# Backward loads in pieces of up to 512 KB instead of 256 KB, and a padded weight loaded from a copy

## The chip, the cores and the metric

The kernel runs on one core of one Trainium2 chip. The metric is the device time of one execution in microseconds (us). A profile is one execution taken by the hardware profiler; its span can differ by some us from the timed runs of the same kernel. Kernels sent together ran on one chip and share its runs of the kernel before; across those chips the median of the kernel before was 1447.5, 1449.6, 1453.8 and 1451.4 us, so kernels of different groups are compared by their ratios. A ratio is the mean time of one kernel's fast runs over that of the kernel before in the same rounds, so it is not quite the ratio of the medians quoted beside it.

Engines: PE multiplies matrices (PEld is its weight load), DVE, ACT and POOL work element by element, SP issues most DMAs. The 16 DMA engines move the data.

## The reference, cut to what matters

A block with attention and a gated feed-forward network side by side, in bf16, and all its gradients: S = 2048 tokens, D = 448, 16 heads of 28, F = 1792.

```python
xn = layernorm(x)
out = x + mha(xn, wqkv, wo) + (silu(xn @ w_gate) * (xn @ w_up)) @ w_down
# returned: out and, for a given grad_out, the gradients of
# x, wqkv, wo, w_gate, w_up, w_down
```

## The kernel before: the parts that the change and the argument touch

The forward (to about 610 us) computes attention and the feed-forward net and stores what the backward will need in DRAM: q, k and the like (QD_d, KD_d), feed-forward tiles (F_d), attention output (OT_d), transposed weights (wT_d). The backward then runs 512 attention steps. Each needs PE (two score and two gradient matmuls, four accumulating ones), ACT (two exponentials) and DVE (two products, the ds tile). Between the steps PE is filled with other units: y (the output of the block), dx (gradient through the feed-forward net), dc (through the projections).

All loads of the backward are issued by one queue, SP, between the DMA transposes of ds:

```python
RATE = 100 << 10                        # bytes a step

def drip(key, pieces, due):             # put pieces on the waiting list
    slow.extend((due, key, o, i) for o, i in pieces)
    slow.sort(key=lambda x: x[0])

def drop():                             # once a step
    # ... rate = RATE, or more where a piece is due soon
    credit += rate
    while slow and credit > 0:
        _, _, o, i = slow.pop(0)
        SP.dma_start(out=o, in_=i)
        credit -= size(o)

def load_q(g, qc):
    t = new_q(g, qc)                    # [P, 4, 512] bf16, 512 KB
    drip(("q", g, qc), [(t[:, i:i + 2], QD_d[g, qc, :, i:i + 2]) for i in (0, 2)], 128 * g + 4 * qc - 4)

def dst_dma(b, ds, qi):                 # three of four steps: transpose by DMA
    if qi == 0:
        dsT[b] = bk.tile([P, 4, 2, 4, P], BF16, name="dsT", bufs=3)
    SP.dma_start_transpose(out=dsT[b][:, qi].rearrange("p j kt s -> p (j kt) s"),
                           in_=ds[:].rearrange("p j k -> p (j k)"))
# ... the ds of the fourth step is transposed by PE and copied by ACT
# ds_sb has 10 buffers; y has 2
```

The weight wo is needed with each head of 28 rows padded to 32. The kernel before loads it in the backward in four DMAs of 28 partitions, into a tile that POOL clears first. The forward had built the same padded layout in SBUF once already (wo_pad).

The softmax here doesn't subtract the row's maximum and nothing guards it: scores larger than these inputs give would overflow.

## Time and profile before

| | kernel before |
|---|---|
| time | 1447.26 us (1446.37 to 1447.65, 3 runs) |
| profiled span | 1448.2 us |
| PE, ACT, DVE busy | 92%, 87%, 80% |
| DMA packets, bytes | 701763, 271.18 MB |
| plain DMAs and transposes on SP | 558 and 505 (compiled order) |

The busy row of an engine says how long it ran instructions, the waits say what ended its idle time. The DMA row is the mean share of time in which each of the 16 engines had a packet under way; packets overlap, so it can pass 1. The lines themselves are shown in the prediction.

### The profile page before, as it was taken

The page shows a single profiled execution, that of the slowest core. Times are in us where ns is not written, and L with a number is a line of the kernel's source. Part 1 is how long each engine was busy: PE and PEld are TensorE (multiplying, and loading weights), DVE is VectorE, ACT ScalarE, POOL GpSimd, SP SyncE. Part 2 cuts the span into 40 slices and gives each one's busy share as a digit, 9 for nine tenths or more (in the row PEclk, how much of TensorE's full clock was granted, in tenths as well). Part 3 has the DMA queues.
Part 4 walks back from the last instruction along what each step waited for, and adds up shares of the span by engine and source line. Part 5 has one row for each costly group of instructions (what it writes and reads, how often), then busy time and mean ns, then how long its engine had stood idle before and what let it go on. Part 6 is the DMA issues. An engine that isn't in the chain of part 4 may idle for free. (4 is left out here: it accounts for less than half of the span.)

```text
span 1448.2 us, 34787 instructions
## 1 busy us (share of the span) xinstructions
PE 1335.4 (92%) x12708; PEld 539.9 (37%) x12708; DVE 1151.7 (80%) x1997; ACT 1261.2 (87%) x2193; POOL 363.1 (25%) x486
## 2 busy tenths in 40 slices
PE   5899999999999999889899989999999999999996
PEld 2333333333333333333333433433343344443343
DVE  6677756666667666488898988888889999989988
ACT  5788988988999999778898988899989999989974
POOL 6475514453344453110101101101001011010005
PEclk9999999999999999989999999999999999999998
DMA  6797947796778676799999999999999999999971
GB/s 153 161 211 184 220 112 166 177 203 154 157 170 184 143 175 145 193 211 204 217 218 211 208 225 181 211 211 212 232 193 192 208 215 230 199 197 201 204 145 60
DMA packets 701763, 271.18 MB, mean 187 GB/s; under 512 B 620224, under 2 KB 676248, under 8 KB 701592
## 3 DMA queue, kind: packets, MB, share of 16 engines
q1 hardware_dynamic: 696616, 262.83, 88.5%
q0 software_dynamic: 3568, 5.83, 1.8%
q8 instruction: 100, 1.64, 0.5%
q14 instruction: 71, 0.58, 0.1%
q10 hardware_dynamic: 1408, 0.30, 0.1%
HBM read 65.04 MB, written 59.90 MB: 86 GB/s over the span
## 5 line engine op out<-in xcount | busy, mean ns | idle before, releaser
L840 DVE TENSOR_TENSOR ds_sb<-db,e_sb 128x512 bf16<-128x512 f32 x1024 | 646.8, 684 | 54.7 <-issue 25.5
L834 ACT ACTIVATE e_sb<-sb 128x512 bf16<-128x512 f32 x1024 | 555.0, 612 | 66.1 <-PE db L818 49.8
L611 ACT ACTIVATE eT<-s_w 128x1024 bf16<-128x1024 f32 x256 | 263.5, 1029 | 47.0 <-PE s_ps L608 44.0
L613 ACT ACTIVATE eT<-s_ps 128x512 bf16<-128x512 f32 x512 | 280.5, 613 | 0.0
L818 PE MATMUL db<-kd,qd 32*128 32x512 bf16 x1024 | 236.1, 385 | 7.2 <-DVE ds_sb L840 6.4
L810 PE MATMUL sb<-kd,qd 32*128 32x512 bf16 x1024 | 210.7, 388 | 7.4 <-DMA qd<-QD_d 3.5
L959 POOL TENSOR_TENSOR dq_acc<-dq_acc,dq_st 128x256 f32<-128x256 f32 x64 | 46.4, 726 | 571.6 <-ACT dq_st L957 571.6
L917 PE MATMUL acc<-ds_sb,qd 128*32 128x512 bf16 x1024 | 161.1, 391 | 0.0
L913 PE MATMUL acc<-e_sb,qd 128*32 128x512 bf16 x1024 | 159.0, 391 | 1.3 <-DVE dw_o L527 1.3
L900 ACT COPY dsT<-db 128x1024 bf16<-128x1024 bf16 x128 | 130.2, 1017 | 14.1 <-PE db L895 13.5
L379 POOL TENSOR_TENSOR nn<-nn,ag 128x512 f32<-128x512 f32 x56 | 71.2, 1271 | 249.6 <-DVE ag L377 240.9
L608 PE MATMUL s_ps<-QQ,KK 32*128 32x512 bf16 x512 | 125.3, 385 | 3.9
L1127 PE MATMUL genb<-wguT,dau_c 128*128 128x448 bf16 x448 | 117.5, 355 | 6.3 <-ACT dq_st L957 3.9
L608 PE MATMUL s_w<-QQ,KK 32*128 32x512 bf16 x512 | 100.3, 387 | 11.8 <-ACT eT L611 10.2
L810 PEld LDWEIGHTS <-qd 32*128 32x128 bf16 x1024 | 48.2, 91 | 152.4 <-issue 140.6
L420 PE MATMUL gen<-xn_t,f_sp 128*128 128x448 bf16 x416 | 91.8, 354 | 2.6 <-DVE nn L394 1.7
L944 PE MATMUL genb<-dsT,kd 128*32 128x256 bf16 x2048 | 79.1, 274 | 6.0 <-DVE y L1079 4.2
L420 PEld LDWEIGHTS <-f_sp 128*128 128x128 bf16 x640 | 55.7, 98 | 75.9 <-issue 32.0
L895 PE MATMUL db<-ident_bf,ds_sb 128*128 128x128 bf16 x1032 | 79.0, 220 | 1.1 <-DVE ds_sb L840 1.1
L895 PEld LDWEIGHTS <-ds_sb 128*128 128x128 bf16 x1032 | 67.9, 98 | 24.6 <-issue 6.0
L380 POOL TENSOR_TENSOR nn<-nn,tt 128x512 f32<-128x512 f32 x56 | 72.0, 1286 | 4.4
L450 PE MATMUL gen<-eT,VS 128*32 128x512 bf16 x1024 | 68.4, 384 | 4.3 <-DVE nn L394 2.2
(163 smaller groups left out, 1879.5 us busy)
## 6 DMA issues: line engine op xcount, KB each, us to landing
F_d<-hda SPq DMA_DIRECT2D x56, 384.0 KB
dau_c<-F_d SPq DMA_DIRECT2D x56, 256.0 KB
h_c<-F_d SPq DMA_DIRECT2D x24, 256.0 KB
qd<-QD_d SPq DMA_DIRECT2D x24, 256.0 KB
dsT<-ds_sb SPq DMA_TRANSPOSE x383
dc<-dqkvT_d SPq DMA_DIRECT2D x12, 384.0 KB
wT_d<-wT_f SPq DMA_DIRECT2D x14, 256.0 KB
KD_d<-qk_sp SPq DMA_DIRECT2D x7, 512.0 KB
```

The costliest lines, as they stand in the source:

```text
L420: PE.matmul(ps[:, :D], lhsT=fsp[fc][:, t // 4, w, t % 4, :], rhs=rhs[:, t, :], start=(t == 0), stop=(t == NT - 1))
L608: PE.matmul(sp4[hh], lhsT=KK[g][r:r + HP, kt * P:(kt + 1) * P], rhs=QQ[g][r:r + HP, qsl], start=True, stop=True, tile_position=(r, 0))
L611: ACTE.activation(out=e2[0][:], in_=wide[:], func=ACT.Exp, scale=SCALE)
L613: ACTE.activation(out=e2[1][:, j], in_=sp4[2 + j], func=ACT.Exp, scale=SCALE)
L810: PE.matmul(s_ps[:], lhsT=qside[g, qc][r:r + HP, 0, qi * P:(qi + 1) * P], rhs=kside[g, kc][r:r + HP, 0, :], start=True, stop=True, tile_po ...
L818: PE.matmul(d_ps[:], lhsT=qside[g, qc][r:r + HP, 1, qi * P:(qi + 1) * P], rhs=kside[g, kc][r:r + HP, 1, :], start=True, stop=True, tile_po ...
L834: ACTE.activation(out=est[k][:, j], in_=sps.pop((k, j))[:], func=ACT.Exp, scale=SCALE)
L840: DVE.tensor_tensor(out=ds[:, j], in0=dps.pop((k - 1, j))[:], in1=est[k - 1][:, j], op=ALU.mult)
L895: PE.transpose(ps[:, c, :], ds[:, c // 4, (c % 4) * P:(c % 4 + 1) * P], ident_bf[:])
L900: ACTE.copy(out=o, in_=ps[:])
L913: PE.matmul(a[r:r + HP, :], lhsT=sp4[:, 1, r:r + HP], rhs=e[:, j, :], start=first, stop=last, tile_position=(0, r), skip_group_check=True)
L917: PE.matmul(a[r:r + HP, :], lhsT=sp4[:, 0, r:r + HP], rhs=ds[:, j, :], start=first, stop=last, tile_position=(0, r), skip_group_check=True)
```

## The change

Its intent: fewer and larger transfers, as the DMA row is full in the backward, with no change to the order of any compute engine. Pieces of 256 KB become pieces of up to 512 KB; wo is stored once, padded, in the forward, and comes back in one DMA. Cut to its core:

```diff
+    wo_d = dram.tile([P, G, D], BF16)
 ...
         if k == 13:
             woT_load(3)
+            SP.dma_start(out=wo_d[:], in_=wo_pad[:, :, :D])
 ...
-        drip(("q", g, qc), [(t[:, i:i + 2], QD_d[g, qc, :, i:i + 2]) for i in (0, 2)], 128 * g + 4 * qc - 4)
+        drip(("q", g, qc), [(t[:], QD_d[g, qc])], 128 * g + 4 * qc - 4)
 ...  (k, fT, x_c, o_c, wd and wguT alike)
-                               for a, b in ((0, 2), (2, 4), (4, 6), (6, 7))], due)      # h_c
+                               for a, b in ((0, 4), (4, 7))], due)
-    POOL.memset(wo_sb[:], 0.0)
-    drip(("y", 0, 1), [(wo_sb[HP * pv(hh):HP * pv(hh) + DH, :, :], wo_v[hh]) for hh in range(4)], 50)
+    drip(("y", 0, 1), [(wo_sb[:], wo_d[:])], 50)
-        drip(("dx", ch, fq), [(d[:, i - f0], F_d[ch, :, i, 1:3, :]) for i in range(f0, f1)], now + 16)
+        drip(("dx", ch, fq), [(d[:, i - f0:min(i + 2, f1) - f0], F_d[ch, :, i:min(i + 2, f1), 1:3, :]) for i in range(f0, f1, 2)], now + 16)
```

More of the change, by code (lines that the diff above doesn't have):

```diff
@@ L776, in load_q @@
         t = new_q(g, qc)
-        drip(("q", g, qc), [(t[:, i:i + 2], QD_d[g, qc, :, i:i + 2]) for i in (0, 2)], 128 * g + 4 * qc - 4)
+        drip(("q", g, qc), [(t[:], QD_d[g, qc])], 128 * g + 4 * qc - 4)
     def load_k(g, kc):
         t = new_k(g, kc)
-        drip(("k", g, kc), [(t[:, 0:2], KD_d[g, kc, :, 0:2]), (t[:, 2], KD_d[g, kc, :, 2])], 128 * g + 16 * kc - 4)
+        drip(("k", g, kc), [(t[:], KD_d[g, kc])], 128 * g + 16 * kc - 4)
     steps = [(g, hp, kc, qc, qi) for g in range(G) for hp in range(2) for kc in range(4)
@@ L871 @@
     w2 = bk.tile([P, 4, 2, P], BF16, name="dqT", bufs=1)
-    drip(("f",), [(fT[:, sc], fT_d[:, sc]) for sc in range(4)], 10)
+    drip(("f",), [(fT[:, a:a + 2], fT_d[:, a:a + 2]) for a in (0, 2)], 10)
     def late_dw(c):
@@ L1038, in load_y @@
             x_c = yp.tile([P, 4, D], BF16, name="x_c")
-            drip(("y", ch, half), [(x_c[:, a:a + 2], x_d[:, 4 * ch + a:4 * ch + a + 2, :]) for a in (0, 2)], due)
+            drip(("y", ch, half), [(x_c[:], x_d[:, 4 * ch:4 * ch + 4, :])], due)
             ych[ch, 2] = x_c
@@ L1042, in load_y @@
             o_c = yp.tile([P, G, 512], BF16, name="o_c")
-            drip(("y", ch, half), [(o_c[:, a:a + 2], OT_d[ch, :, a:a + 2]) for a in (0, 2)], due)
+            drip(("y", ch, half), [(o_c[:], OT_d[ch])], due)
             ych[ch, 3] = o_c
@@ L1047 @@
     wo_sb = yp.tile([P, G, D], BF16, name="wo_sb", bufs=1)
-    POOL.memset(wo_sb[:], 0.0)
     wd_v = B_w_down.rearrange("(fc p) d -> p fc d", p=P)
-    drip(("y", 0, 0), [(wd_sb[:, a:a + 2, :], wd_v[:, a:a + 2, :]) for a in (0, 2, 4, 6)], 35)
+    drip(("y", 0, 0), [(wd_sb[:, a:a + 4, :], wd_v[:, a:a + 4, :]) for a in (0, 4)], 35)
     load_y(0, 0)
     load_k(0, 2)
-    drip(("y", 0, 1), [(wd_sb[:, a:a + 2, :], wd_v[:, a:a + 2, :]) for a in (8, 10, 12)], 50)
-    drip(("y", 0, 1), [(wo_sb[HP * pv(hh):HP * pv(hh) + DH, :, :], wo_v[hh]) for hh in range(4)], 50)
+    drip(("y", 0, 1), [(wd_sb[:, a:a + 3, :], wd_v[:, a:a + 3, :]) for a in (8, 11)], 50)
+    drip(("y", 0, 1), [(wo_sb[:], wo_d[:])], 50)
     load_y(0, 1)
@@ L1104, in load_w @@
         w = dxs["w", fq] = dxs["pool"].tile([P, 5, 2, D], BF16, name="wguT")
-        drip(("dx", 0, fq), [(w[:, i - f0], wT_d[:, i, :, :D]) for i in range(f0, f1)], due)
+        drip(("dx", 0, fq), [(w[:, i - f0:min(i + 2, f1) - f0], wT_d[:, i:min(i + 2, f1), :, :D]) for i in range(f0, f1, 2)], due)
     def load_dx(ch, fq):
```

## The prediction

> **What bounds the kernel now.** I read the busy times and the 40 slices first, then the busy time by stretch, then who waits for a DMA, then the DMA queue's own rows. The chain that ended last is no help: it covers the final 1.5 us only.
>
> ```profile
> PE 1335.4 (92%) x12708; PEld 539.9 (37%) x12708; DVE 1151.7 (80%) x1997; ACT 1261.2 (87%) x2193; POOL 363.1 (25%) x486
> PE   5899999999999999889899989999999999999996
> DMA  6797947796778676799999999999999999999971
> ```
>
> The reader sees two rows at 9: PE from start to end, and the mean of the 16 DMA engines from slice 18 on, where the backward begins. That second row is what the change aims at, so I took the backward apart (columns: stretch, length, busy us of PE, PEld, DVE, ACT, POOL, granted clock, DMA share, GB/s):
>
> ```profile
> 650.00:700.00 50.00, 45.92 (x495) 17.53 (x492) 42.09 (x69) 43.74 (x83) 4.35 (x6) 0.93 1.06 205
> 950.00:1000.00 50.00, 47.60 (x536) 19.44 (x534) 40.76 (x66) 47.39 (x93) 4.36 (x6) 1.00 1.15 220
> 600.00:1400.00 800.00, 751.86 (x8492) 313.24 (x8492) 711.10 (x1192) 714.99 (x1329) 67.83 (x94) 0.99 1.07 206
> ```
>
> From 600 to 1400 us PE is busy 752 of 800 us (94%), with ACT and DVE at 89%. The DMA share is 1.07: packets overlap in time, so a share over 1 says that the engines always have work queued, not that anyone waits. Who waits is in the wait view (us in total, times, longest), from which these are all the waits of compute engines for DMAs in the backward:
>
> ```profile
> DVE y L1079 <- DMA out_dram<-y: 5.7, 3, 2.3
> DVE ds_sb L840 <- DMA dsT<-ds_sb: 5.0, 6, 1.7
> PEld L810 <- DMA qd<-QD_d: 3.6, 1, 3.6
> PE sb L810 <- DMA qd<-QD_d: 3.5, 1, 3.5
> PEld L810 <- DMA kd<-KD_d: 2.5, 1, 2.5
> PE sb L810 <- DMA kd<-KD_d: 2.0, 1, 2.0
> PEld L1071 <- DMA o_c<-OT_d: 1.3, 1, 1.3
> PEld L944 <- DMA dsT<-ds_sb: 1.2, 2, 0.9
> PE genb L1071 <- DMA o_c<-OT_d: 0.8, 1, 0.8
> PEld L1071 <- DMA dsT<-ds_sb: 0.4, 1, 0.4
> PEld L810 <- DMA dsT<-ds_sb: 0.4, 1, 0.4
> ```
>
> PE lost 3.5 + 2.0 + 0.8 = 6.3 us to DMAs, the 3.5 of it at the very turn (before 625 us) on a load that the change leaves as it is. DVE lost 10.7 us, all between 640 and 900 us; from 900 us on only 0.4 us of a weight load's wait is left. So although the DMA row is full, **PE with ACT and DVE close behind** bounds the backward, and DMA is a full but tolerated second.
>
> Last the queue that issues: is SP late?
>
> ```profile
> SPq L827 <- DVE ds_sb L840: 270.8, 244, 2.5
> SPq L827 <- PE db L818: 97.9, 86, 2.9
> L827 SPq DMA_TRANSPOSE dsT<-ds_sb x383: 1231/1267/3143, 624.3 to 1400.5; - x192
> L767 SPq DMA_DIRECT2D dau_c<-F_d x56: 421/572/1197, 913.6 to 1243.1; - x56
> ```
>
> The rows give min/median/max ns of one issue. A transpose holds the queue 1.27 us, a load 0.57 us. But the two waits ahead say that the queue stood 369 us waiting for the ds tile that the next transpose reads: it keeps pace with the compute and has room.
>
> **What the Trainium skill says.** "Perfetto Trace Analysis", section "DMA Optimizations", says that larger DMAs use memory bandwidth better and that DMAs under 2 KB have large overhead, but also that splitting lets some start sooner. The first is the change's intent; the second is what it gives up. "DMA: Bandwidth & Descriptors", section "Why small descriptors are slow (HBM only)", gives about 3 cycles a packet beside one per 32 bytes: estimated from that page, 67 cycles against 64 at 2 KB and 131 against 128 at 4 KB, so 2 KB to 4 KB saves some 2%. No row of the trace before shows it. "Issuing engines are not separate DMA queues" on the same page has all DMAs interleave on the same 16 engines: a transpose shares them with a load, whatever its size. The trace agrees that transposes get late when loads are heavy (DVE waits 5.0 us for ds_sb to be read, only during 640 to 900 us).
>
> **The change part by part.** I compared the compiled instruction order of both kernels. PE (25288 rows), DVE (1032) and ACT (1152) are the same row for row; POOL loses one row; SP goes from 1065 to 978 DMAs. So nothing moves on the bounding engines, only the times at which data is there.
>
> 1. *Fewer issues.* Loads: dau_c 56 to 32, h_c 32 to 16, kd 28 to 14, qd 24 to 12, wguT 14 to 8, o_c 8 to 4, x_c 8 to 4, wd 7 to 4, fT 4 to 2, wo 4 to 1; and one store more. That is 88 less and 1 more: 87 x 0.57 us = 50 us of the SP queue. All of it lies beside other work: SP waits 369 us for producers, and will wait some 50 us more. On the path: 0.
>
> 2. *The same bytes.* Only qd, kd, o_c and fT get longer contiguous runs per partition (2 KB to 4 KB; kd 2 + 1 to 3). They are 24 x 256 KB + 14 x 384 KB + 8 x 256 KB + 4 x 256 KB = 14.2 MB, a twentieth of the 271 MB moved; h_c keeps runs of 1 KB, dau_c of 2 KB, wd and x_c of 0.9 KB. At 2% that is 14.2 MB / 206 GB/s x 0.02 = 1.4 us of DMA time over the whole backward. On the path: under 1.
>
> 3. *When a load is complete.* The drip sends a piece as soon as its credit is above zero and then goes into debt, so a whole tile goes out where its first half went before. Counting dsT transposes ahead of each load, most tiles are complete 1 to 3 transposes earlier (a transpose each 2 us: 776 us / 383). The kd load that PE waits 2.0 us for (at 843.5 us; its second piece issued only at 841.1) had 101 and 102 transposes ahead, and now has 100; the o_c load of the 0.8 us wait is likewise complete some two transposes earlier. Both waits should go: 2.0 + 0.8 = 2.8 us at most, on PE.
>
> 4. *What stands behind a larger piece.* At 206 GB/s 256 KB take 1.27 us and 512 KB 2.54 us, so a transpose, a store of y or a small load queued behind one can land 1.3 us later, half as often. The dsT tile is read at least 9 steps after its transposes are issued, (1400 - 615) / 512 = 1.53 us each, or 14 us: hidden. The tight places are the 6 ds_sb and 3 y waits on DVE, 10.7 us. They could grow by 1.3 us each, 9 x 1.3 = 12 us on DVE, or shrink, as the mean traffic is equal. DVE has 11% of slack, so I take +1 us on the end.
>
> 5. *wo.* The four loads of 28 partitions (98 KB each, 0.9 KB runs) become one of 448 KB over 128 partitions with 3.5 KB runs: four issues of 0.39 us to one, no wait on either. The POOL memset of 1.61 us at 626 us goes; POOL is idle there and nobody waited for it. The new store of 448 KB is issued at about 65 us, next to the last woT transpose; there the DMA share is 1.02 at 214 GB/s, so it takes 459 KB / 214 GB/s = 2.1 us and can hold up the weight transpose behind it. PE is busy 16.75 of 20 us there. I take +0.3 us.
>
> Sum: 0 - 0.5 - 2.8 + 1 + 0.3 = -2.0 us: 1447.26 - 2.0 = **1445 us**.
>
> **The rivals.** (a) *The DMA engines are the real bound*: share 1.07 to 1.15, and if large pieces were much cheaper the backward would shorten as a whole. Against it: the waits above, and that PE is at 95% precisely where the share is 1.15. If all the 6.3 + 10.7 us went, and PE got all of it, 1430 us. (b) *Bursts delay transposes*: 512 KB at once ahead of tight waits; for it, those waits exist already. All 12 us of step 4 on the path would give 1458; more only if PE starts to wait for dsT, which the 14 us of lead speak against. (c) *All hidden*: every wait moves to another place and the end stays at 1447. That is close to my own answer.
>
> **Range and chances.** I choose 1445, with 1438 (DVE's waits shrink too) to 1453 (half of rival b). A change of 2% needs 29 us. That is more than all DMA waits taken together, so faster gets 0.02; slower needs a new steady wait for transposes, 0.02; within 2%, 0.96.
>
> **What would show it.** Right: SP with 87 fewer DMAs and longer waits for ds_sb; PE's kd and o_c waits gone; PE's busy time between 600 and 1400 us unchanged, about 752; DMA share still over 1. Step 4 shows in DVE's waits on dsT and y, between 5 and 20 us. Wrong: PE waiting for dsT for tens of us, or the DMA share clearly lower with the span shorter by as much, would say that the transfers bounded it after all; a later start of the backward (first row of L810 now at 614.6 us) by over 2 us would say that step 5 was mis-sized.

## The result, and the profile after

The changed kernel took 1447.89 us (1447.69 to 1448.04, 4 runs) beside 1447.45 us for the kernel before on the same chip (1446.37 to 1451.47, 4 runs): ratio 0.9998, 95% interval 0.9979 to 1.0017. It is the same time. The profiled span was 1445.9 us.

The busy rows in 40 slices, and the busy time by stretch, of the changed kernel:

```profile
PE   5899999989999999889898999999999999999996
DMA  5897857696778676799999999999999999999971
```

```profile
650.00:700.00 50.00, 46.17 (x493) 18.07 (x492) 42.53 (x70) 44.39 (x84) 4.78 (x7) 0.90 1.13 213
950.00:1000.00 50.00, 47.62 (x552) 19.80 (x555) 41.32 (x66) 47.73 (x93) 4.36 (x6) 1.00 1.14 210
600.00:1400.00 800.00, 753.41 (x8495) 315.68 (x8496) 713.11 (x1195) 715.25 (x1328) 66.17 (x93) 0.98 1.07 206
```

The last row matches the one of before in every column: PE 753 us against 752, DMA share 1.07 and 206 GB/s in both. The DMA engines were not relieved at all. (Some 60 matmul records are missing from this trace, which its page shows as 12647 of 12708; the tenths of a slice may differ for that alone.) The waits for DMAs after the turn to the backward:

```profile
DVE y L1080 <- DMA out_dram<-y: 7.5, 3, 4.4
PEld L812 <- DMA qd<-QD_d: 3.7, 1, 3.7
PE sb L812 <- DMA qd<-QD_d: 3.5, 1, 3.5
...
DVE ds_sb L842 <- DMA dsT<-ds_sb: 1.9, 2, 1.4
...
PE genb L881 <- DMA dsp<-fT_d: 1.2, 1, 1.2
```

PE's waits for kd (2.0 us) and o_c (0.8 us) are gone. A wait of 1.2 us for fT, which now comes in two pieces of 512 KB instead of four of 256 KB, is new; that the pieces cause it is not shown, as the run with the pieces alone (below) does not have it. DVE's two waits are 9.4 us together, 10.7 before. Last, the queue:

```profile
SPq L829 <- DVE ds_sb L842: 316.7, 248, 3.4
SPq L829 <- PE db L820: 97.0, 93, 2.1
```

The waits for the next ds tile grew from 271 to 317 us: the issue time that was saved is spent waiting. So far the trace agrees with the prediction. It does not yet say how near the queue and the DMA engines are to being the limit. That is what the experiments are for.

### The profile page after: what moved, and what is told of

Its sections match the earlier page's. It is cut to its first block, busy times and chain, and to the rows that moved or that the text cites. A ratio compares the mean times of both kernels' runs of the same rounds, so it can differ in the third digit from the quotient of the medians.

```text
span 1445.9 us, 34634 instructions
## 1 busy us (share of the span) xinstructions
PE 1329.5 (92%) x12647; PEld 542.9 (38%) x12708; DVE 1151.6 (80%) x1997; ACT 1262.1 (87%) x2193; POOL 361.5 (25%) x485
```

## The experiments

Theory: compute (PE, with ACT and DVE behind) sets the pace of the backward, and the transfers are hidden behind it. Rivals: the DMA engines bound it; the SP queue bounds it; larger pieces cost as much by their bursts as they save. No experiment takes compute away, so the theory is tested only by ruling out the rivals. Twelve kernels ran, all with three timed rounds; all gave the right result but one.

| kernel | plain DMAs on SP | time, us | ratio to before | 95% interval |
|---|---|---|---|---|
| before | 558 | 1447 to 1454 | 1 | |
| changed | 471 | 1447.9 | 0.9998 | 0.9979 to 1.0017 |
| larger pieces alone | 473 | 1449.9 | 1.0008 | 0.9974 to 1.0043 |
| wo part alone | 556 | 1450.9 | 1.0005 | 0.9983 to 1.0026 |
| pieces of 112 to 128 KB | 715 | 1521.8 | 1.0486 | 1.0452 to 1.0519 |
| whole tiles, to 1.25 MB | 435 | 1452.3 | 1.0019 | 0.9999 to 1.0039 |
| 12 MB of loads less | 463 | 1448.4 | 0.9961 | 0.9936 to 0.9987 |
| 33 MB more, 128 copies | 599 | 1525.0 | 1.0489 | 1.0446 to 1.0532 |
| 67 MB more, 256 copies | 727 | 1618.1 | 1.1140 | 1.1109 to 1.1170 |
| four buffers for y | 471 | 1452.1 | 0.9984 | 0.9955 to 1.0013 |
| changed + 256 issues of 8 KB | 727 | 1544.8 | 1.0639 | 1.0607 to 1.0671 |
| before + 256 issues of 8 KB | 814 | 1576.6 | 1.0858 | 1.0825 to 1.0891 |
| 33 MB more, 32 copies | 503 | 1543.3 | 1.0642 | 1.0607 to 1.0677 |
| before, runs of 1 KB | 566 | 1452.9 | 1.0009 | 0.9984 to 1.0034 |

### One part at a time: the pieces alone, and wo alone

Edit: the changed kernel without its wo lines, and the kernel before with only those.

> The larger pieces alone; wo as before (four loads of 28 partitions, memset, no store in the forward). Theory (compute bounds the backward, all but some us of the transfers are hidden): 1447, within 0.3% of the kernel before, PE's kd and o_c waits gone as in the changed kernel. Rival bursts: if large pieces cost something that the wo part gives back, this is 2 to 10 us slower than before. Rival DMA-bound: faster by over 5 us here, the wo part taking it back.

> The wo part alone; pieces as before. Theory: 1447 within 0.3%; the 448 KB store at about 65 us costs at most 2 us of the forward, and the one load instead of four changes nothing. Rival: if the store delays the weight transposes of the forward, the first backward matmul starts over 2 us later than 614.6 us and the end is later by as much.

Ratios 1.0008 and 1.0005: neither part moves the time by more than its interval (0.4% at most), so no gain of one beyond that is given back by the other. With wo alone the kd wait of 2.0 us is there as before, and with the pieces alone it is gone: the pieces did it. The first backward matmul started at 615.9 us (pieces) and 610.8 us (wo); over the profiles of all kernels, most with one and the same forward, it lies between 610.8 and 618.3 us. A delay of 2 us by the store in the forward can therefore not be seen in one profile, and the timed runs, with an interval of 0.2% or 3 us each way, cannot tell it either.

### Smaller pieces

Edit, in the changed kernel (k, fT, h_c, x_c, o_c, wd, wguT and dau_c alike):

```diff
-        drip(("q", g, qc), [(t[:], QD_d[g, qc])], 128 * g + 4 * qc - 4)
+        drip(("q", g, qc), [(t[:, i], QD_d[g, qc, :, i]) for i in range(4)], 128 * g + 4 * qc - 4)
```

> The changed kernel with every drip load cut to pieces of 64 to 128 KB: some 190 more issues than in the kernel before. Theory: SP has over 300 us of waits in the backward and absorbs 190 x 0.57 = 108 us; time 1447 to 1452, SP's waits for ds_sb down by some 100 us. Rival DMA-bound (small transfers cost DMA time): 1460 or more, and DMA waits on PE. Rival SP-bound: PE and DVE wait for dsT, 1460 or more.

Measured 1521.8 us, ratio 1.0486: my theory, which gave at most 1452, missed. (The pieces are in fact 112 to 128 KB, and the issues 157 more than in the kernel before, not 190.) The bytes are the same, so piece size does matter, only not from 256 KB upwards. The queue's rows in order of time show how (start, length in us, instruction, count; neighbours of one kind are merged, idle time between them included). First the changed kernel:

```profile
1009.47 3.22 SPq L829 DMA_TRANSPOSE dsT<-ds_sb  x2
1012.75 0.56 SPq L769 DMA_DIRECT2D qd<-QD_d  x1
1013.42 1.25 SPq L829 DMA_TRANSPOSE dsT<-ds_sb  x1
1014.72 0.72 SPq L769 DMA_DIRECT2D dau_c<-F_d  x1
1015.55 6.85 SPq L829 DMA_TRANSPOSE dsT<-ds_sb  x3
```

and the same place with the small pieces:

```profile
1002.14 1.24 SPq L829 DMA_TRANSPOSE dsT<-ds_sb  x1
1003.43 0.63 SPq L769 DMA_DIRECT2D dau_c<-F_d  x1
1004.15 1.24 SPq L829 DMA_TRANSPOSE dsT<-ds_sb  x1
1005.43 0.68 SPq L769 DMA_DIRECT2D dau_c<-F_d  x1
1006.21 1.24 SPq L829 DMA_TRANSPOSE dsT<-ds_sb  x1
1007.50 1.07 SPq L769 DMA_DIRECT2D dau_c<-F_d  x2
1008.68 1.24 SPq L829 DMA_TRANSPOSE dsT<-ds_sb  x1
```

Above, three transposes take 6.85 us, nearly twice the shortest 1.23 us each: they wait for their ds tile. Below, each takes 1.24 us and the next issue follows at once: the tiles are there, and the transposes stand in line behind loads. That is so in this stretch, not everywhere: over the whole run SP still waited 233 us for ds tiles, 84 us less than in the changed kernel, about as much less as expected; only the time was not.

```profile
SPq L829 <- DVE ds_sb L842: 232.6, 217, 3.1
```

The compute engines then wait for what comes late:

```profile
DVE ds_sb L842 <- DMA dsT<-ds_sb: 36.9, 23, 3.0
PEld L1128 <- DMA dau_c<-F_d: 15.2, 12, 2.1
PE genb L1128 <- DMA dau_c<-F_d: 11.2, 11, 1.9
```

And the DMA engines had less to do than before, not more:

```profile
600.00:1400.00 800.00, 711.18 (x7683) 292.14 (x7679) 644.85 (x1081) 650.55 (x1203) 60.14 (x84) 0.94 1.01 189
```

A share of 1.01 at 189 GB/s, where it was 1.07 at 206. "Perfetto Trace Analysis" of the Trainium skill, section "Optimizing DMA Performance", counts an issuing sequencer whose track is solid DMA slices as one way of being DMA-bound. This stretch looks so. But the sign alone does not tell: from 640 to 1400 us SP's rows cover 701 of 760 us here, and 692 in the kernel before and 690 in the changed one, which lost nothing. Of the 463 us that SP waited in that window of the changed kernel, 448 lie inside such rows by the trace's semaphore events, so a row covers waiting as well as issuing.

The granted clock was 0.94 from 600 to 1400 us here, 0.98 in the changed kernel. Whether the lower clock added to the loss was not tested.

### More issues, or shorter runs?

Small pieces bring two things at once: 157 more plain DMAs than the kernel before, and runs (the contiguous bytes of one partition) of 1 KB in place of 2 KB. Two kernels take them apart. Edits:

```diff
 # changed kernel, and likewise the kernel before
+            if bk is not None and k % 2 == 1:
+                SP.dma_start(out=tiny_d[k // 2][:], in_=QD_d[0, 0, :, 0, 0:32])
 # kernel before, as many pieces of the same size
-        drip(("q", g, qc), [(t[:, i:i + 2], QD_d[g, qc, :, i:i + 2]) for i in (0, 2)], ...)
+        drip(("q", g, qc), [(t[:, i::2], QD_d[g, qc, :, i::2]) for i in (0, 1)], ...)
```

> The changed kernel with 256 extra issues of 8 KB each (128 rows of 64 B, memory to memory, 2 MB in all), one at every second step. 727 plain DMAs on the queue, as many as with the small pieces (715), but the loads stay large. Theory A (the issue queue is the limit that the small pieces hit): 256 x 0.57 = 146 us more issue time, so 1500 to 1540 like the small pieces. Theory B (short pieces are slow in the DMA engines): 1447 to 1455, since almost no bytes are added.

> The kernel before with the same 256 extra issues. Theory A: the change freed 50 us of issue time that stayed idle, so here, with the queue as the limit, the kernel before is 40 to 60 us slower than the changed kernel with the same load: the headroom the change made. Theory B: both the same to 5 us.

> The kernel before with as many loads (566 plain DMAs against 558) of the same sizes, but each made of runs of 1 KB per partition instead of 2 KB (qd, kd, o_c, fT, dau_c). Theory A: within 0.5% of before. Theory B: 1480 to 1520, most of what the small pieces lost.

Runs of 1 KB cost nothing: 1.0009, with nearly as many packets (715459) as the small pieces have (718045). The tiny issues cost 1.0639 in the changed kernel, at 727 plain DMAs, where the small pieces cost 1.0486 at 715. (1544.8 us is a little above the 1500 to 1540 expected.) So the number of issues explains the loss and the run length does not. What was not tested is the same DMAs issued by another engine; that would tell the time on SP's queue from any other cost of one more DMA. The tiny ones are also of another kind than the loads (memory to memory, rows of 64 B). The DMA engines were again not the fuller for it:

```profile
600.00:1400.00 800.00, 710.15 (x7584) 289.45 (x7583) 633.65 (x1063) 644.95 (x1190) 60.15 (x84) 0.94 0.98 189
```

Each tiny DMA held the queue 0.58 us (median), 256 of them 149 us, and the time grew by some 97 us (1544.8 - 1447.9, from two chips): about a third of the added issue time was absorbed.

The same load on the kernel before gave 1576.6 us, 32 us more than on the changed kernel. Here, with the queue as the limit, the 87 issues that the change saves (50 us by the prediction's step 1) are worth 32 us, under the 40 to 60 expected. That is where the saved issue time of the change went: **into room on a queue that was not yet the limit.**

### How near is the limit of the queue?

From the first to the last DMA transpose of ds, which are 383 in every kernel, I added up the rows of the plain DMAs and took 1.24 us for each transpose, as when none waits (475 us). The sum is the issue time that the same backward needs; the share is that of the 777 us which this stretch lasts in the changed kernel. This is an estimate from the traces' rows:

| kernel | plain DMAs, their time | issue time needed | share of 777 us | ratio |
|---|---|---|---|---|
| whole tiles (below) | 155, 97 us | 572 us | 74% | 1.0019 |
| changed | 191, 118 us | 593 us | 76% | 0.9998 |
| before | 279, 164 us | 639 us | 82% | 1 |
| before, runs of 1 KB | 287, 174 us | 649 us | 84% | 1.0009 |
| small pieces | 435, 260 us | 735 us | 95% | 1.0486 |
| changed + tiny | 446, 271 us | 746 us | 96% | 1.0639 |
| before + tiny | 534, 320 us | 795 us | 102% | 1.0858 |
| 33 MB more, 32 copies (below) | 223, 142 us | 617 us | 79% | 1.0642 |
| 33 MB more, 128 copies (below) | 319, 198 us | 673 us | 87% | 1.0489 |
| 67 MB more, 256 copies (below) | 446, 281 us | 756 us | 97% | 1.1140 |

In the first seven rows, where the bytes are the same or nearly so, up to 84% no time is lost, and from 95% on much is; where between them it begins was not measured. That the rest up to 100% cannot be used is what the program's order suggests, as a transpose cannot be issued before its ds exists and what is behind it has to wait; this was not tested by itself. The table is an account, not a law: small pieces lose less at 95% than tiny ones do at 96%. The last three rows lose more than their share explains; they follow below.

### Whole tiles in one load

Edit: every tile of the drip in one piece, for instance

```diff
-        drip(("dx", ch, fq), [... for i in range(f0, f1, 2)], now + 16)
+        drip(("dx", ch, fq), [(d[:, 0:f1 - f0], F_d[ch, :, f0:f1, 1:3, :])], now + 16)
```

> Every tile in one load: up to 1.25 MB for dau_c, 0.9 MB for h_c and for the halves of wd, 1.1 MB for wguT. Theory: 1447 within 0.5%. Rival bursts: transposes stand 6 us behind such a load, so DVE's waits for ds_sb and y grow to 20 to 40 us and the time to 1455 to 1475. Rival DMA-bound: faster than the changed kernel by over 5 us.

1452.3 us, ratio 1.0019 (0.9999 to 1.0039). DVE's waits for these DMAs:

```profile
DVE y L1080 <- DMA out_dram<-y: 6.3, 2, 5.3
DVE ds_sb L842 <- DMA dsT<-ds_sb: 3.2, 4, 1.6
```

That is 9.5 us together and so no more than with 512 KB: bursts up to 1.25 MB don't delay the transposes enough to reach the compute. The rival of bursts falls. Nor is anything gained.

### Fewer bytes, and more bytes

Edits in the changed kernel: half of each dau_c and wguT tile and three of seven chunks of h_c are not loaded, and the matmuls read the loaded half twice (a wrong result); or copies from memory to memory are added.

```diff
-                lhsT=d[:, i // 2, i % 2, tsl], rhs=dxs["w", fq][:, i // 2, i % 2, :]
+                lhsT=d[:, i // 2, 0, tsl], rhs=dxs["w", fq][:, i // 2, 0, :]
 # 33 MB in 128 copies of 256 KB; with k % 2 67 MB in 256
+            if bk is not None and k % 4 == 1:
+                SP.dma_start(out=junk_d[k // 4][:], in_=QD_d[0, 0, :, 0:2])
 # 33 MB in 32 copies of 1 MB, runs of 2 KB as well
+            if bk is not None and k % 16 == 9:
+                SP.dma_start(out=junk_d[k // 16] ..., in_=QD_d[0, :, :, 0:2] ...)
```

> The changed kernel, with a wrong result on purpose: the same matmuls, but only half of each dau_c and wguT tile and 4 of 7 chunks of each h_c tile are loaded and the loaded half is read twice. Takes some 12 MB of loads (about 7% of what moves in the backward) away. Theory: 1445 to 1447, DMA share down by 0.05, the waits of DVE for stores of y smaller. Rival DMA-bound: 12 MB / 206 GB/s = 58 us less DMA work, so faster by 20 us or more.

> The changed kernel with an extra copy of 256 KB from memory to memory (runs of 2 KB) at every fourth step of the backward, 33 MB in all, about 20% more bytes. Theory: the DMA engines have some room left although their share reads over 1; time 1447 to 1470. Rival DMA-bound: at 206 GB/s this is 160 us more DMA work, so 1550 or more.

> The same with a copy at every second step, 67 MB, about 40% more. Theory: somewhere the room ends; 1500 to 1650, with PE and DVE waiting for dsT by then. Rival DMA-bound: about 320 us more, 1700 or more. If even this stays at 1450, the DMA share says nothing on room.

> The changed kernel with the 33 MB of the run with 20% extra bytes, in the same runs of 2 KB, but in 32 copies of 1 MB instead of 128 of 256 KB: the bytes with a quarter of the issues. Theory A: below 1475, the loss of 72 us having been mostly issue time. Theory B: 1510 or more, as the bytes are the same.

Fewer bytes, window 600 to 1400 us:

```profile
600.00:1400.00 800.00, 757.03 (x8498) 316.70 (x8496) 710.49 (x1190) 718.41 (x1331) 66.22 (x93) 0.98 1.01 192
```

The DMA share fell from 1.07 to 1.01, and the time by 0.4% against the kernel before (ratio 0.9961), some 6 us, where a DMA-bound backward would have given 20 or more. So the kernel is not bound by its DMA engines.

More bytes did cost: 33 MB in 128 copies 1.0489 (1525 us, between the 1470 at most of my theory and the 1550 at least of the rival, so neither was right), in 32 copies 1.0642. My expectation for the second, below 1475 us because the loss of the first would be issue time, was wrong. With 32 copies the queue needs 617 of 777 us by the account above, 79%, less than in the kernel before, and the time still rose. SP waited for ds as long as in the changed kernel (325 us beside 317), not less as with too many issues (233 and 213). Its waits and its window:

```profile
SPq L830 <- DVE ds_sb L843: 325.2, 216, 5.4
600.00:1400.00 800.00, 709.84 (x7591) 287.46 (x7590) 635.09 (x1065) 645.66 (x1191) 60.16 (x84) 0.94 1.10 223
```

Share 1.10 at 223 GB/s: here more is moved per us than before, while with too many issues it was less (189). This is a second limit, on the side of the bytes. It shows in the transposes too: from the end of its row to its landing one took 2.7, 2.9 and 3.0 us (medians of the 40 to 55 in each trace whose landing is known) with 128, 32 and 256 copies, beside 2.3 us in the changed kernel and 2.1 and 2.2 us with the small pieces and the tiny issues. Whether it is the DMA engines or the memory is not told: the copies read and write memory, where a load only reads it. With 256 copies, 67 MB and 240 GB/s the ratio was 1.1140, against 1.0639 for as many issues with 2 MB: the bytes cost on top of the issues. Why the same 33 MB cost more in large copies than in small ones was not settled; the two ran on different chips, and a burst of 1 MB ahead of the transposes is only a guess: their landing is a little later (2.9 us beside 2.7), but loads of up to 1.25 MB did not have that effect (2.2 us with whole tiles).

### Four buffers for y

Edit: `y = yp.tile([P, D], BF16, name="y", bufs=4)` in the changed kernel.

> The changed kernel with four buffers for y instead of two, so that DVE need not wait for the store of an earlier y. Theory: DVE's 7.5 us on y vanish and with them PE's 5.6 us behind y; 1 to 5 us faster than the changed kernel. Rival (all hidden, ACT or PE bounds there anyway): the same to 1 us.

DVE's wait for the stores of y vanished, and its waits for ds_sb to be read rose to 8.0 us in that profile. Ratio 0.9984 (0.9955 to 1.0013): not told from 1. The 1 to 5 us of my theory are not seen, though the interval leaves room for them. A wait on an engine with slack need not be time. No version with a right result beats both kernels beyond doubt.

## Why the prediction was right or wrong

The time (1447.9 us) lies in the predicted range of 1438 to 1453, and "within 2%" was right. By its steps:

1. *Fewer issues, none on the path.* Right in the sum: 87 DMAs less (the traces have 1063 and 976 on SP, two fewer each than the prediction counts), SP's waits for ds longer by 46 us, no time gained. But its ground, "it keeps pace with the compute and has room", was mis-sized. It took the 369 us of waits for room. Nearly all waits of SP lie inside the rows of issues (415 of 429 us from 640 to 1400 us), so they can't be added to them: 650 us of issue (383 x 1.27 and 285 or so x 0.57) and 369 us of waits are over 1000 us, in a backward of 785. By the account above the kernel before has some 138 us to spare (777 - 639). The tiny issues measured how much of such room is of use: 149 us more of issue in the changed kernel cost some 97 us, so about 50 us were absorbed.
2. *The same bytes.* Right. (The tiles with longer runs are 14592 KB, which is 14.9 MB in the unit of the 271 MB and not 14.2; nothing changes by it.) The share and the GB/s of the backward are unchanged, and halving the runs instead of doubling them gave 1.0009.
3. *When a load is complete.* Right in the mechanism: the kd and o_c waits are gone. The size stays open: -2.8 us of the time is too small to be seen. In this trace a new wait of 1.2 us for fT gives part back, and the rest is below what the runs resolve.
4. *What stands behind a larger piece.* Right: DVE's waits are 9.4 us, inside the 5 to 20 foretold, and stayed at 9.5 with pieces up to 1.25 MB.
5. *wo.* Right that it is nothing within 0.2 to 0.3% (1.0005); the +0.3 us itself is too small to be seen. The test proposed for it, a first backward matmul later by 2 us, was too fine: that start moves by 7 us between profiles.

That the time came within 3 us of the 1445 is partly luck: each term of the sum is smaller than what the runs resolve, and 1447, no change at all, fits as well. One reading of the lines was wrong: a DMA share over 1 does not say "that the engines always have work queued". Counted from the traces, fewer than 16 packets were under way in 22% of the time from 640 to 1400 us in both kernels, so at least one of the 16 engines was then free.

Rival (a), the DMA engines as the real bound, is refuted as a bound (fewer bytes: 0.4%) but was close: a fifth more bytes cost 5 to 6%. Rival (b), bursts, fell with whole tiles at 1.0019. Rival (c), all hidden, is what happened. What the prediction did not see is that queue and transfers stand close behind compute (no loss at 84% of the issue time, 5% at 95%; 5 to 6% lost with a fifth more bytes), so that the same change is worth nothing in one direction while its opposite costs 5%.

## What to carry to other kernels

That a change gives no time doesn't mean that its resource is free: try the opposite change too. Here 256 KB to 512 KB gave nothing and 256 KB to 128 KB cost 5%, because the queue had just enough room. Add up what a queue must issue (count by shortest duration) instead of trusting its row, which reads full in every kernel, or the sum of its waits, which lies inside those rows.

## What the Trainium skill lacked or had wrong

- "DMA: Bandwidth & Descriptors", section "Issuing engines are not separate DMA queues", calls a sequencer's time for issuing "usually small relative to the DMA itself". For one DMA that holds here too (0.58 us of issue, 3.9 us from issue to landing, medians of the added copies of 256 KB). In sum it does not stay small: SP needs 76 to 82% of the backward for issuing, and 256 more issues of 8 KB cost 6.4%.
- The same page gives no time of an issue in us for this chip, only cycle counts of "previous generations" in a comparison. The traces show that the size does not matter for plain DMAs (median 0.58 us for 8 KB, 0.57 for 256 KB, 0.58 for 1 to 1.25 MB), and 1.23 us at the shortest for a 256 KB transpose from SBUF to SBUF. This sets what one queue can do.
- The same page, section "Rules for kernel authors", asks for 1 MiB per DMA for bandwidth. From 256 KB to 512 KB the ratio was 0.9998, and to 1.25 MB 1.0019; in this kernel, which bandwidth does not bound, the size of the loads mattered only through the number of issues.
- "Perfetto Trace Analysis", section "DMA Optimizations", warns of DMAs under 2 KB. Halving the runs to 1 KB per partition, the DMAs staying at 128 to 256 KB, gave 1.0009; the page does not say whether it means the run or the transfer.
- "Perfetto Trace Analysis", section "Optimizing DMA Performance", takes a sequencer's solid track as the sign of its being the limit. SP's rows covered 91% of 640 to 1400 us in the two kernels that lost nothing and 92% with the small pieces. What differed was the sum of SP's waits for ds (272 us before, 317 changed, 233 with small pieces, 213 with tiny issues). The median length of a transpose does not tell either (1.27 us before, 1.24 with small pieces, 1.27 with tiny issues).
